# Attention and gated MLP on one core: how ScalarE and VectorE share the PSUM banks of the score blocks

## The chip, the cores and the metric

The kernel runs on one core of a Trainium2 chip. The metric is the device time of one execution in microseconds. Before the change the median of 14 runs is 795.35 us (791.35 to 800.95).

## The reference, cut to what matters

Two branches read the same `x` (2048 tokens of 512): an attention with 32 query heads of 16 that share one key and one value head, and a gated MLP with a 2048 x 2048 mixing matrix over the tokens. A sigmoid gate per token mixes them.

```python
q = (x @ wq) as 32 heads of 16;  k = x @ wk;  v = x @ wv        # one k and one v for all heads
scores = einsum('bhqd,bkd->bhqk', q, k) * 16 ** -0.5             # 32 x 2048 x 2048
a = softmax(scores) @ v  -> [2048, 512] @ wo
z = gelu(x @ w_in);  z1 = z[..., :688];  z2 = layernorm(z[..., 688:])
b = (z1 * (w_sp @ z2 + b_sp)) @ w_out
out = g * a + (1 - g) * b            # g = sigmoid((x * gate_w).sum(-1))
```

## The kernel before, in words

**Score blocks.** The attention is cut into 32 units of 64 score blocks, 2048 in all. A block is 128 keys x 512 columns, one PSUM bank of float32. Its matmul contracts over 32 rows only and uses one of the four row groups of the TensorE array (`s_mm`, recorded at L286); blocks of different row groups that stand next to each other run together. A *burst* is a group of such matmuls written for one exp.

**Two engines turn scores into weights.** ScalarE takes several banks at once and writes exp as bfloat16 to a slot of `P` (`exp_op`, L575; seven slots). VectorE takes one bank at a time: `d_A` (L599, "dA") evacuates it as an affine function in float16 to `X`, and for each batch of four blocks six polynomial steps on 1,024 columns follow (`d_poly`: square L607, add L609, square L611, each twice). VectorE's blocks thus get a polynomial in place of exp, and a small correction per unit (the `MC` and `CC` matmuls) adds what is missing. Which block goes to which engine is not fixed by hand.

**P times V.** TensorE multiplies the weights of either engine with `V` into bank 6 (`pv_mm`, L286, 128*32 tiles), four column groups beside each other. At the end of a unit VectorE transposes bank 6 (L623), and GpSimd divides by the sums (L629 to L635).

**The rest.** All projections, the mixing matmuls and the output go through bank 7 with an evacuation by VectorE (`Group` objects; L469, L476, L358, L523, L552 and others). ScalarE's gelus come in one piece near 272 us (L484, L508). To keep TensorE's clock up, matmuls on `ones` that nobody reads are put in where its load is low (`keep_pick`).

**PSUM.** Eight banks of 512 columns. Before the change, banks 0 to 2 and 3 to 4 are ScalarE's two slots, filled in turn with three and with two blocks; bank 5 (`BD`) is VectorE's; 6 (`BO`) is P times V and 7 (`BM`) everything else. Bank 5 also serves one of the last output tiles.

**Who sets the order.** A planner written in Python runs while the kernel is built. It follows TensorE, ScalarE and VectorE with a cost for each operation, asks `pe_pick`, `act_pick` and `dve_pick` for what could run next, and takes the ready candidate of the lowest priority number. The order that comes out is fixed for each engine; on the chip the engines wait for each other by semaphores, and every engine works strictly in that order. TensorE's candidates are: a ScalarE burst (priority 0, once the exp two bursts back is done), a lone VectorE block (1, unless a ScalarE burst is due within `SOON` = 300 ns), P times V (2, or 0.5 under pressure) and the groups (3). If bank 5 is free when a ScalarE burst is emitted, VectorE's block is put behind it. `dve_pick` takes evacuations first (0), then the unit ends (1) and small work (2), then dA (3), then the polynomial steps (4).

A batch for VectorE is taken from the upper end of a unit's key blocks, ScalarE takes them from the lower end, and at most 28 of the 64 blocks of a unit can go to VectorE (`NMAX`, `RMIN`).

Of the kernel before, what the change touches and what calls it, by code (L numbers as in the profile page):

```python
# [7 lines left out]
ACT = mybir.ActivationFunctionType  # L8
# [31 lines left out]
RLAST = 14  # L40
PVMIN = 8
PRESS = 1
SOON = 300
KEEP = 7.5
LOW = 6.0
MMARG = 250.0
# [106 lines left out]
def build_kernel(nc, x_d, wq_d, wk_d, wv_d, wo_d, win_d, wsp_d, bsp_d, wout_d, gw_d, out_d):  # L153
    es = ExitStack()
    with es:
# [7 lines left out]
        def bank(b, n=512, off=0):  # L163
            return ps[:, 512 * b + off:512 * b + off + n]

        BD = 5
        BO = 6
        BM = 7
        EB = ((0, 3), (3, 2))

        def bkey(b):
            return ("sc", 0) if b < 3 else ("sc", 1) if b < 5 else ("bk", b)

        xT = sb("xT", [128, 4, S], B16)
        wq = sb("wq", [128, 4, D], B16)
# [395 lines left out]
               rk + [("Q", (u // 2) % NQ)], [bkey(b)], tp=(32 * g, 0), tag="S")  # L571

        def exp_op(k, n):
            b0, _ = EB[k % 2]
            op("act", lambda a: a.activation(P[:, k % NP, 0:512 * n], ps[:, 512 * b0:512 * (b0 + n)], ACT.Exp),  # L575
               r=[("sc", k % 2)], w=[("P", k % NP)], tag="exp")

        pvn = {}

# [15 lines left out]

        pvt = {}

        def d_A(m, i):
            op("dve", lambda v: v.tensor_scalar(X[:, m % NX, 512 * i:512 * i + 512], bank(BD), PA, PB, ALU.mult, ALU.add),  # L599
               r=[("bk", BD)], w=[("X", m % NX, i * 2 // DB)], tag="dA")  # L600

        def d_poly(m):
            res = []
# [60 lines left out]


        for i in range(12):
            mm(bank(3 + i % 2), ones[:, 0:128], ones[:], True, True, ["ones"], [("sc", 1)], tag="warm")
        for dt in range(4):
            k_mm(0, dt, BM)
        k_ev(0, BM)  # L670
        for dt in range(4):
            q_mm(0, dt, BD)
        op("act", lambda a: a.activation(QA[:, 0, :], bank(BD), ACT.Copy), r=[("bk", BD)], w=[("Q", 0)], tag="Qev")
        op("dve", lambda v: v.tensor_scalar(wvg[:, :, 16:32], wk_sb[:], 0.25, None, ALU.mult), r=["wk"], w=["wvk"])
        op("dve", lambda v: v.tensor_copy(gw_rep[:], wvg[:, :, 32:33].broadcast_to([128, 4, 128])), r=["gw"], w=["gwr"])
        op("dve", lambda v: v.tensor_scalar(nmf[:], pidx[:], 0.0, None, ALU.is_ge), r=["pidx"], w=["nmf"])
# [36 lines left out]
        order = [(n // 4, n % 4) for n in range(64)]  # L713
        st_ = {"ua": 0, "kf": 0, "ke": 0, "pu": 0}
        stepb, sdone, edone, slot_left = {}, {}, {-1: 0.0, -2: 0.0}, {}
        dbank = {"free": 9500.0, "blk": None, "ready": None}
        batches = []
        cur = {"m": None, "gs": []}
        pd_left, bdone, xfree = {}, {}, {}
# [41 lines left out]
        def d_block(now, used):  # L761

            if not cur["gs"] and not new_batch(now):
                return None
            m = cur["m"]
            u, kt = batches[m]
            fr = [g for g in cur["gs"] if g not in used]
            if used and not fr:
                return None
            g = fr[0] if fr else cur["gs"][0]  # L770

            def take():
                cur["gs"].remove(g)
                i = cur["i"]
                cur["i"] += 1
                s_mm(BD, (u, kt, g))
                dbank["blk"] = (m, i, (u, kt, g))
            return take

        def sw(kind):  # L780
# [2 lines left out]
        def pe_pick(now):  # L783
            k = st_["kf"]
            ua = unit_for_act()
            cands = []
            dfree = dbank["blk"] is None and dbank["free"] + LAT <= now
            soon = False
            if ua < NU and edone.get(k - 2) is not None:
                nb = EB[k % 2][1]  # L790
                bl = []
                t = edone[k - 2] + (LAT if k >= 2 else 0)
                u = ua
                lo = units[u]["lo"]
                while len(bl) < nb and u < NU:
                    if lo >= units[u]["hi"]:
                        u += 1
                        if u < NU:
                            lo = units[u]["lo"]
                        continue  # L800
                    kt, g = order[lo]
                    r = when(("Q", u // 2), ("K", 0, kt // 4) if u % 2 == 0 else "K1")
                    if r is None:
                        break
                    if bl and r > max(t, now):
                        break
                    t = max(t, r)
                    bl.append((u, kt, g))
                    lo += 1
                if bl:  # L810
                    soon = t < now + SOON

                    def emit():
                        T["now"] = now
                        for i_, blk in enumerate(bl):
                            s_mm(EB[k % 2][0] + i_, blk)
                            units[blk[0]]["lo"] += 1
                        stepb[k] = bl
                        st_["kf"] += 1
                        unit_for_act()  # L820
                        if dfree:
                            tk = d_block(now, [b[2] for b in bl])
                            if tk:
                                tk()
                                dbank["new"] = True

                    def fin(t_end):
                        sdone[k] = t_end + LAT
                        if dbank.pop("new", None):
                            dbank["ready"] = t_end + LAT  # L830
                    cands.append((t, 0, sw("S") + 226, emit, fin, "S"))

            if dbank["blk"] is None and not soon:
                tk = d_block(now, ())
                if tk:
                    def fin2(t_end):
                        dbank["ready"] = t_end + LAT
                    cands.append((dbank["free"] + LAT, 1, sw("S") + 216, tk, fin2, "S"))

            pu = st_["pu"]  # L840
            if pu < NU:
# [105 lines left out]

        last_pe = {"kind": ""}
        tl_state = {12: 0, 13: 0}
        tl_bank = {12: BM, 13: BD}  # L950

        def keep_pick(now):

            while load and load[0][0] < now - 3400:
                load.popleft()
            have = sum(w_ for _, w_ in load)
            if have >= KEEP or st_["pu"] >= NU:
                return None
            if misc["cur"] is None and misc["free"] + LAT <= now and not tl_state[12]:
                b = BM  # L960
            elif dbank["blk"] is None and dbank["free"] + LAT <= now and not tl_state[13]:
                b = BD
            else:
                return None

            def emit():
                after = [pg.ops["dve"][-1]] if gel_on and gel else []
                mm(bank(b), ones[:, 0:128], ones[:], True, True, ["ones"], [("bk", b)], tag="keep", after=after)
            return (now, 1.5 if have < LOW else 9, C512 + sw("M"), emit, None, "M")

        def tail_pick(now):

            if st_["ua"] < NU - 2 or main or fins or ns or qs or misc["cur"] is not None or when(("OT", 3, 2), *[("u", ft, 3) for ft in range(6)]) is None:
                return None
            for t2 in (12, 13):
                if tl_state[t2] >= 9:
                    continue
                if t2 == 12:
                    ok = misc["free"] + LAT <= now
                else:  # L980
                    ok = st_["ua"] >= NU and not cur["gs"] and dbank["blk"] is None and dbank["free"] + LAT <= now
                if not ok:
                    continue

                def emit():
                    i = tl_state[t2]
                    if i < 6:
                        yb_mm(t2, i, tl_bank[t2])
                    else:
                        wo_mm(t2, i - 6, tl_bank[t2])  # L990
                    tl_state[t2] += 1
                return (now, 3, C512 + sw("M"), emit, None, "M")
            return None
# [67 lines left out]
        def dve_pick(now):  # L1061
            cands = []
            for q, pr in ((evac_q, 0), (norm_q, 1), (dve_q, 2)):
                if q:
# [11 lines left out]
                        if d_:  # L1076
                            d_(t_end + LAT)
                    cands.append((t, pr, c_, e, f))
            if dbank["blk"] is not None and dbank["ready"] is not None:
                m, i_, blk = dbank["blk"]  # L1080

                def e1():
                    d_A(m, i_)
                    bblk.setdefault(m, []).append(blk)

                def f1(t_end):
                    dbank["blk"] = None
                    dbank["ready"] = None
                    dbank["free"] = t_end
                    if i_ == DB - 1:  # L1090
                        ops_ = d_poly(m)
                        for z, (c_, f_) in enumerate(ops_):
                            polyq.append((c_, f_, m, z - 4 if z >= 4 else None))
                cands.append((dbank["ready"], 3, 601, e1, f1))
            if polyq:
                cp_, fp_, mp, last = polyq[0]

# [21 lines left out]
        while True:  # L1119
# [25 lines left out]
                if idle_rounds > 300:  # L1145
                    break
            free[eng] = min(nxt + [now + 200.0])
        assert st_["pu"] == NU and not (first or qs or ns or main or fins or gel or dve_q or evac_q or norm_q or polyq or act_q), \
            (st_, len(first), len(qs), len(ns), len(main), len(fins), len(gel), len(dve_q), len(evac_q), len(norm_q), len(polyq))
        if INFO is not None:  # L1150
            print({"est": tend, "busy": busy, "batches": len(batches), "n": [(64 - u["hi"]) // 4 for u in units], "tail": (tl_state, tl_bank)}, nc.sbuf_bytes_remaining)
# [5 lines left out]
                else:  # L1157
                    wo_mm(t2, i - 6, tl_bank[t2])
        for t2 in (14, 15):
            tl_bank[t2] = EB[st_["kf"] % 2][0] + (t2 - 14)  # L1160
        for t2 in (14, 12, 15, 13):
            wo_mm(t2, 3, tl_bank[t2], first=t2 >= 14)
        for t2 in (14, 12, 15, 13):
# [172 lines left out]
```

## Time and profile before

| what | value |
|---|---|
| median of 14 runs | 795.35 us |
| profiled execution | 792.48 us, span 790.7 us |
| granted TensorE clock | 0.993 |
| TensorE busy | 721.0 us (91%) |
| VectorE busy | 737.9 us (93%) |
| ScalarE busy | 765.6 us (97%) |
| first exp starts, last exp ends | 10.2 us, 781.0 us |

The span is from the first to the last instruction; the execution's own time is 1.8 us longer. PE is TensorE's matmul, PEld its weight load, DVE VectorE, ACT ScalarE, POOL GpSimd. A group's line gives line, engine, operation, output<-input, shapes and count; then busy time and mean duration of one; then the idle time of the engine just before them and what ended it. On ScalarE and VectorE an instruction's row overlaps the next one's by about 0.1 us, so sums of durations exceed busy times.

### The profile page before, as it was taken

To read this page: it belongs to the slowest core of one execution; us is meant where nothing else is said; L and a number is where in the kernel's file an instruction comes from. 1 tells how busy PE (TensorE), PEld (TensorE's weight loads), DVE (VectorE), ACT (ScalarE), POOL (GpSimd) and SP (SyncE) were. 2 spreads that over 40 slices of the span, in tenths; PEclk is the share of its full clock that TensorE was granted. 3 is DMA by queue.
4 is the path that set the end of the run, shared out by engine and by line. 5 is a ranking of instruction groups with operands and counts; after the bars stand their busy time and mean duration, and the time that the engine had idled before them with its cause. 6 is when DMAs were issued, how large, how long until landed. Compare 5 with 4: busy or idle time off the path is not lost.

```text
span 790.7 us, 13960 instructions
## 1 busy us (share of the span) xinstructions
PE 721.0 (91%) x5356; PEld 203.7 (26%) x5448; DVE 737.9 (93%) x1370; ACT 765.6 (97%) x669; POOL 135.7 (17%) x111
## 2 busy tenths in 40 slices
PE   7889999898999878999999999999999999999997
PEld 2222222222222222222222222222222222222221
DVE  3789999999999999999999899999999999899996
ACT  5999999999999999999999999999999999999995
POOL 3111101221120104211012111101112211111220
PEclk9899999999999999999999999999999999999999
DMA  9710000000000000000050000041000023000000
GB/s 192 171 28 1 1 1 1 1 1 2 1 1 1 2 0 1 1 1 1 1 121 15 1 1 1 1 81 47 7 2 1 1 54 68 14 1 2 2 1 30
DMA packets 49050, 16.99 MB, mean 21 GB/s; under 512 B 44130, under 2 KB 48914, under 8 KB 48979
## 3 DMA queue, kind: packets, MB, share of 16 engines
q1 hardware_dynamic: 46066, 15.10, 9.0%
q10 hardware_dynamic: 2784, 0.69, 0.5%
q8 instruction: 44, 0.72, 0.4%
q0 software_dynamic: 128, 0.26, 0.2%
q14 instruction: 28, 0.22, 0.1%
HBM read 3.20 MB, written 2.10 MB: 7 GB/s over the span
## 4 chain that ended last, share of the span: by engine, by line
PE 36%; DVE 28%; ACT 21%; issue 14%; DMA 1%; SPq 0%; ACTq 0%; DVEq 0%
PE ps L286 24%; ACT P L575 20%; PE ps L285 12%; DVE X L599 10%; DVE X L607 4%; DVE X L611 3%; DVE X L609 3%; DVE bst L490 2%; DMA xT<-in_A_x_dram 1%; DVE z L469 1%; DVE z L476 1%; DVE z L500 1%; DVE T L623 1%; DVE mv L492 0%; DVE OT L638 0%
## 5 line engine op out<-in xcount | busy, mean ns | idle before, releaser
L575 ACT ACTIVATE P<-ps 128x1536 bf16<-128x1536 f32 (+1 forms) x648 | 739.4, 1286 | 8.8 <-PE ps L286 7.1
L286 PE MATMUL ps<-QA,KA 32*128 32x512 bf16 x2048 | 335.7, 385 | 42.0 <-ACT P L575 23.3
L599 DVE TENSOR_SCALAR X<-ps 128x512 f16<-128x512 f32 x428 | 290.6, 679 | 25.4 <-PE ps L286 24.5
L629 POOL TENSOR_TENSOR rc<-T,mone 128x16 f32<-128x16 f32 x31 | 93.5, 3018 | 565.6 <-DVE T L623 565.6
L286 PE MATMUL ps<-P,V 128*32 128x512 bf16 x1620 | 160.8, 386 | 1.1 <-issue 0.8
L286 PEld LDWEIGHTS ps<-QA,KA 32*128 32x128 bf16 x2048 | 84.1, 91 | 300.1 <-ACT P L575 189.0
L611 DVE TENSOR_TENSOR X<-X 128x1024 bf16<-128x1024 f16 x214 | 144.4, 687 | 0.0
L607 DVE TENSOR_TENSOR X<-X 128x1024 f16<-128x1024 f16 x214 | 142.5, 685 | 0.0
L285 PE MATMUL ps<-wT,z 128*128 128x512 bf16 x348 | 108.5, 384 | 2.5 <-issue 2.1
L609 DVE TENSOR_SCALAR X<-X 128x1024 f16<-128x1024 f16 x214 | 85.4, 425 | 0.0
L286 PE MATMUL ps<-X,V 128*32 128x512 bf16 x428 | 69.9, 385 | 0.3 <-DVE T L623 0.2
L286 PEld LDWEIGHTS ps<-P,V 128*32 128x32 bf16 x1620 | 33.0, 94 | 60.0 <-issue 58.0
L285 PEld LDWEIGHTS ps<-wT,z 128*128 128x128 bf16 x384 | 29.4, 97 | 64.1 <-issue 55.5
L285 PE MATMUL ps<-ones 128*128 128x512 bf16 x101 | 34.9, 418 | 10.1 <-DVE bst L490 3.8
L285 PE MATMUL ps<-win,xT 128*128 128x344 bf16 x128 | 29.9, 314 | 1.0 <-DVE z L476 0.7
L285 PE MATMUL ps<-wout,z 128*128 128x512 bf16 x84 | 27.8, 385 | 1.1 <-issue 0.8
L285 PE MATMUL ps<-xT,win 128*128 128x512 bf16 x84 | 27.4, 385 | 0.7 <-issue 0.5
L623 DVE STREAM_TRANSPOSE T<-ps 128x512 f32<-128x512 f32 x32 | 22.6, 706 | 2.2 <-PE ps L286 2.2
L635 POOL TENSOR_TENSOR Tn<-T,rcg 128x256 bf16<-128x256 f32 x31 | 20.8, 670 | 2.4
L285 PE MATMUL ps<-xT,wq 128*128 128x512 bf16 x56 | 19.3, 397 | 0.8 <-issue 0.6
L285 PEld LDWEIGHTS ps<-ones 128*128 128x128 bf16 x113 | 10.3, 102 | 36.4 <-DVE bst L490 11.2
L286 PEld LDWEIGHTS ps<-X,V 128*32 128x32 bf16 x428 | 15.9, 94 | 14.3 <-issue 10.9
(102 smaller groups left out, 304.2 us busy)
## 6 DMA issues: line engine op xcount, KB each, us to landing
out_dram<-outsb SPq DMA_DIRECT2D x15, 128.0 KB, 2.2
win<-in_B_w_in_dram SPq DMA_DIRECT2D x2, 688.0 KB, 5.6
wout<-in_B_w_out_dram SPq DMA_DIRECT2D x1, 640.0 KB, 9.0
wo<-in_A_wo_dram SPq DMA_DIRECT2D x1, 512.0 KB, 6.7
wq<-in_A_wq_dram ACTq DMA_DIRECT2D x1, 384.0 KB, 9.3
wT<-in_B_w_sp_dram SPq DMA_TRANSPOSE x16, 4.6
KA<-KA POOLq DMA_DIRECT2D x4, 64.0 KB, 3.8
wq<-in_A_wq_dram ACTq DMA_DIRECT2D x1, 128.0 KB, 4.0
```

Source lines behind the costliest of these rows:

```text
L285: return t.matmul(dst, lhsT, rhs, start=start, stop=stop)
L286: return t.matmul(dst, lhsT, rhs, start=start, stop=stop, tile_position=tp)
L469: ev = lambda: op("dve", lambda v: v.tensor_copy(z1[:, ft, 512 * tc:512 * tc + 512], bank(BM)), r=[BMK], w=[("z1", ft)], tag="z1ev")
L490: dve_q.append((520, lambda st=st, h=h: op("dve", lambda v: v.bn_stats(bst[:, st, h, :], z2[:, FH * st + 344 * h:FH * st + 344 * h + 344]) ...
L575: op("act", lambda a: a.activation(P[:, k % NP, 0:512 * n], ps[:, 512 * b0:512 * (b0 + n)], ACT.Exp), r=[("sc", k % 2)], w=[("P", k % NP)] ...
L599: op("dve", lambda v: v.tensor_scalar(X[:, m % NX, 512 * i:512 * i + 512], bank(BD), PA, PB, ALU.mult, ALU.add), r=[("bk", BD)], w=[("X", ...
L607: res.append((C2, lambda x=x, k=k: op("dve", lambda v: v.tensor_tensor(x, x, x, ALU.mult), r=[k], w=[k], tag="dU")))
L609: res.append((C4, lambda x=x, k=k: op("dve", lambda v: v.tensor_scalar(x, x, PC, None, ALU.add), r=[k], w=[k], tag="dV")))
L611: res.append((C2, lambda x=x, k=k, p_=p_, kp=kp: op("dve", lambda v: v.tensor_tensor(p_, x, x, ALU.mult), r=[k], w=[kp], tag="dW")))
L623: o("dve", lambda v: v.transpose(T1[:], bank(BO)), r=[("bk", BO)], w=["T1"], tag="T1")
L629: o("pool", lambda g: g.tensor_tensor(rc[:].unsqueeze(2), lsum, mone[:].unsqueeze(2), ALU.pow), r=["T1", "mone"], w=["rc"], tag="rc")
L635: o(e, lambda v: v.tensor_tensor(tn, t1[:, :, 0:16], s_[:].unsqueeze(2).broadcast_to([128, 16, 16]), ALU.mult), r=["T1", k], w=[("Tn", pr, ...
```

## The change

Banks 0 to 2 and 3 to 5 become two slots of three banks, filled in turn. Each bank has its own key for the waits; before, the banks of a slot had one in common. A burst always has three blocks. When it is emitted and VectorE has at most `DAQ` = 1 evacuations and at most `DPQ` = 8 polynomial steps queued, the third bank of the slot is given to a VectorE block of another row group, and the exp has two banks; otherwise the exp has all three. A slot is filled again when both the exp and, where there was one, the dA of two bursts back are done. Lone VectorE bursts are gone, and `SOON` with them. dA gets priority -1, ahead of all other VectorE work. Keep-alive matmuls use bank 7 alone, and the late output tile takes the third bank of a free slot. Line numbers after L43 move by one at first (L599 becomes L600).

```diff
-SOON = 300
+DAQ = 1
+DPQ = 8
+APRI = -1.0
...
-        BD = 5
-        EB = ((0, 3), (3, 2))
+        EB = (0, 3)
         def bkey(b):
-            return ("sc", 0) if b < 3 else ("sc", 1) if b < 5 else ("bk", b)
+            return ("bk", b)
...
         def exp_op(k, n):
-            b0, _ = EB[k % 2]
+            b0 = EB[k % 2]
             op("act", lambda a: a.activation(P[:, k % NP, 0:512 * n], ps[:, 512 * b0:512 * (b0 + n)], ACT.Exp),
-               r=[("sc", k % 2)], w=[("P", k % NP)], tag="exp")
+               r=[bkey(b0 + i) for i in range(n)], w=[("P", k % NP)], tag="exp")
...
-        def d_A(m, i):
-            op("dve", lambda v: v.tensor_scalar(X[...], bank(BD), PA, PB, ALU.mult, ALU.add), r=[("bk", BD)], ...)
+        def d_A(m, i, b):
+            op("dve", lambda v: v.tensor_scalar(X[...], bank(b), PA, PB, ALU.mult, ALU.add), r=[bkey(b)], ...)
...  # pe_pick
-            if ua < NU and edone.get(k - 2) is not None:
-                nb = EB[k % 2][1]
+            if ua < NU and edone.get(k - 2) is not None and ddone.get(k - 2) is not None:
                 bl = []
-                t = edone[k - 2] + (LAT if k >= 2 else 0)
+                t = max(edone[k - 2], ddone[k - 2]) + (LAT if k >= 2 else 0)
-                while len(bl) < nb and u < NU:
+                while len(bl) < 3 and u < NU:
...
                     def emit():
+                        b0 = EB[k % 2]
+                        tk = None
+                        if len(da_q) <= DAQ and len(polyq) <= DPQ:
+                            tk = d_block(now, [b[2] for b in bl[:2]])
+                        if tk:
+                            del bl[2:]
                         for i_, blk in enumerate(bl):
-                            s_mm(EB[k % 2][0] + i_, blk)
+                            s_mm(b0 + i_, blk)
+                        if tk:
+                            new.append(tk(b0 + 2))
+                        else:
+                            ddone[k] = 0.0
-                        if dfree:
-                            tk = d_block(now, [b[2] for b in bl])
-                            if tk:
-                                tk()
...
-            if dbank["blk"] is None and not soon:
-                tk = d_block(now, ())
-                if tk:
-                    cands.append((dbank["free"] + LAT, 1, sw("S") + 216, tk, fin2, "S"))
...  # dve_pick
-                cands.append((dbank["ready"], 3, 601, e1, f1))
+                cands.append((t, APRI, 601, e1, f1))
```

## The prediction

> **What bounds the kernel now.** I read the page's engine shares first, then the groups kept apart by shape, the waits, one stretch of ScalarE's exps, and the timeline of VectorE beside TensorE. The page:
>
> ```profile
> span 790.7 us, 13960 instructions
> PE 721.0 (91%) x5356; PEld 203.7 (26%) x5448; DVE 737.9 (93%) x1370; ACT 765.6 (97%) x669; POOL 135.7 (17%) x111
> ```
>
> Three engines are nearly full, ScalarE most. The groups:
>
> ```profile
> L575 ACT ACTIVATE P<-ps 128x1536 bf16<-128x1536 f32 x324 | 484.8, 1496 | 8.1 <-PE ps L286 6.6
> L575 ACT ACTIVATE P<-ps 128x1024 bf16<-128x1024 f32 x324 | 348.4, 1075 | 0.7 <-PE ps L286 0.5
> L286 PE MATMUL ps<-QA,KA 32*128 32x512 bf16 x2048 | 335.7, 385 | 42.0 <-ACT P L575 23.3 <-DVE X L599 8.4 <-issue 4.6
> L599 DVE TENSOR_SCALAR X<-ps 128x512 f16<-128x512 f32 x428 | 290.6, 679 | 25.4 <-PE ps L286 24.5
> ```
>
> All 2048 score blocks are there: 324x3 + 324x2 = 1620 on ScalarE, 428 on VectorE. The two exp groups add up to 833 us, more than the span, since one exp's row overlaps the next, so the price of an exp is the distance of starts. In this stretch hardly anything waits:
>
> ```profile
> L575 ACT ACTIVATE P<-ps x20: 1018/1354/1672, 726.0 to 747.5; 128x1536 bf16<-128x1536 f32 x10, 128x1024 bf16<-128x1024 f32 x10
> ```
>
> 19 steps in 21.4 us; single starts in the trace lie 1,330 ns apart after a three-bank exp and 904 after a two-bank one (10x1.330 + 9x0.904 = 21.44). A bank is 426 ns, the fixed part 52. From the first exp (10.2 us) to the end of the last (781.0) ScalarE thus needs 324x2.234 = 723.8 us, plus 23.7 for gelus, table loads and small operations. The remaining 23 us are late starts, which the page mostly hides in the overlap (it shows 8.8 idle). By the starts, 20.0 us of them follow two-bank exps (62 ns on average) and 3.4 follow three-bank ones: after a two-bank exp TensorE has only 904 ns to refill the other slot. In 15.5 of the 20 TensorE reached that burst over 100 ns after the slot was free. ScalarE sets the end; TensorE's arrival sets its waits.
>
> The waits, and VectorE's single bank in the timeline:
>
> ```profile
> PEld ps L286 <- ACT P L575: 189.0, 469, 1.2
> PEld ps L286 <- DVE X L599: 51.8, 155, 1.5
> DVE X L599 <- PE ps L286: 24.5, 34, 2.0
> ```
> ```profile
> 404.69 0.67 DVE L599 TENSOR_SCALAR X<-ps 128x512 f16<-128x512 f32 x1
> 405.42 0.38 PE L286 MATMUL ps<-QA,KA 32*128 32x512 bf16 x1 [0.36 <-DVE X L599]
> 405.84 0.69 DVE L599 TENSOR_SCALAR X<-ps 128x512 f16<-128x512 f32 x1 [0.48 <-PE ps L286]
> 406.45 0.68 DVE L607 TENSOR_TENSOR X<-X 128x1024 f16<-128x1024 f16 x1
> 407.05 0.69 DVE L599 TENSOR_SCALAR X<-ps 128x512 f16<-128x512 f32 x1
> ```
>
> VectorE empties its bank, TensorE refills it with one lone matmul, and VectorE stands idle meanwhile. Its starts are 0.60 us apart (dA 601 ns, the two products 599 each, the sum 332), so a score block costs it 601 + (599+332+599)/2 = 1,366 ns. The least that all its work needs, by such distances, is 724.7 us; it ends at 787.1, so it waits about 61 us: 18 in the first 40 us (mostly for K), 3 in the tail, 41 between. By the starts, 32 of them are ahead of dA (the page shows 25.4).
>
> **ScalarE.** The built order of the changed kernel has 234 exps of three banks and 449 of two, 1600 blocks, with 448 on VectorE. 234x1.330 + 449x0.904 = 717.1 us, against 723.8: -6.7 (20 blocks fewer are -8.5, 35 more fixed parts +1.8). [...]
>
> The floor of the span by ScalarE is 10.2 + 717.1 + 23.7 + 9.7 (what follows the last exp) = 760.7 us, to which late starts come. Short windows grow from 324 to 449. No row shows the new burst, so I bound the loss per window by the nearest ones: 11 ns (that behind three-bank exps), and about 200 (the mean of the windows that were late at all, 94 of 321). I take 52, near the 62 of the same window length, less a sixth for TensorE's relief (next part): 449x0.052 + 2.5 for the long windows = 26, ScalarE's path 787. At 62 ns it is 791; break-even with 790.7 is 61 ns.
>
> **TensorE.** Before, bank 5 was often filled alone: the score matmuls form 852 waves (neighbours in different row groups, which run together), 197 of them a lone bank-5 matmul; after, 682, one such. A lone wave takes 0.31 us to the next kind of work in the timeline: 170x0.31 = -53 us. Keep-alive matmuls rise from 113 to 155, +42x0.31 = +13. Net -40 us, off the path: it buys earlier arrival at bursts, counted above with 10 of 62 ns; between 0 and 48 (62 less the 15.5 of 20.0 us in which TensorE was late) it could be anything, and 10 is nearer to nothing because 40 us are 6% of TensorE's 721. P-V waves stay (599 to 595), as do projections, DMAs, GpSimd and the SP queue. The granted clock is 0.993 and TensorE stays as dense, so nothing is taken for it.
>
> **VectorE.** 20 more blocks: 20x1.366 = +27.3 us, making 752.0 us of work. That must be paid from its 61 us of waits. In the built order the queue of polynomial steps was empty ahead of 113 of 428 dA before, and is empty ahead of 7 of 448 after: with two banks and that backlog it hardly starves. Bounds on what goes: nothing, or all 32 ahead of dA and the some 7 ahead of evacuations (L623, L454, L358, L523, L492). I take 28 of the 32 and 3 of the 7, since where it has a backlog it is full already today, as in this stretch (third pair of columns: DVE busy, operations); that removes 31. The span by VectorE is 790.7 + 27.3 - 31 = 787.
>
> ```profile
> core 0: us, PE busy (x) PEld busy (x) DVE busy (x) ACT busy (x) POOL busy (x), PEclk, DMA share, GB/s
> 60.00:100.00 40.00, 37.12 (x294) 11.25 (x296) 40.00 (x77) 39.35 (x35) 7.68 (x6) 1.00 0.00 1
> ```
>
> The order also moves the tail: two batches of polynomial steps, and not one, follow the last dA, so VectorE and not the last exp leads to the end; this is inside its sum.
>
> **The added wait.** A slot is refilled when both engines have left it. dA runs first of all VectorE work, but not in the middle of an operation: up to 0.60 us late, then 0.68 long, at most 1.28 us after its matmul, beside 0.904 for the exp. The third matmul waits on TensorE, and P-V waves, projections and the next burst stand behind it. ScalarE's own two matmuls go first, so its next exp is covered; if that cover fails the price is the first rival's.
>
> **Sum.** The span ends with the longer path; both give 787 us, -3.7 (-0.5%). The profiled run took 792.48, 1.8 over its span; the median of the runs is 795.35, 2.9 more. 787 + 1.8 + 2.9 = 791.7.
>
> **Rivals.** *A slot tied to two engines (slower).* VectorE at 98% runs behind, TensorE stands in front of a third bank, and the next exp comes late. Place: L287 score matmuls waiting for L600. Price: 449 windows at 80 instead of 52 ns, 760.7 + 35.9 + 2.5 = 799, median 804. It decides from 67 ns on (793.1 us). For it: 51.8 us of weight loads already wait on L599. Against: there are now two banks to wait for. Chance 0.33.
>
> *The waits only move (no change).* VectorE sheds 25 to 29 us of waits instead of 31 and pays 27 for its 20 blocks: 789 to 793, median 794 to 798. For it: VectorE's row cannot shrink, and a block costs it 1,366 ns to save ScalarE 426. Chance 0.12.
>
> *TensorE's relief pays in full (faster still).* Late starts fall to 40 ns per window (ScalarE's path 781) and VectorE sheds 39: 779 to 781, median 784 to 786. Against: both must happen at once. Chance 0.07.
>
> *It doesn't do what it says.* Every burst may be shared, but 234 of 683 are not: 683 blocks would need 683x1.366 = 933 us of VectorE. That is already in the counts.
>
> **Numbers.** The forecast has 0.48. Faster by over 0.3% (about what a measurement of this kernel can tell from no change) needs a span under 788.3: that is the fast rival, 0.07, and 0.38 of the forecast's 0.48, together 0.45. Within 0.3% are the forecast's other 0.10 and 0.10 of the second rival, 0.20. Slower are the first rival and the second's last 0.02, 0.35. The range 784 to 804 runs from the fast rival's time to the slow one's; the forecast's own is 788 (ScalarE's windows at 45 ns and VectorE shedding 35: span 783) to 797 (either path at 792).
>
> **What would show it.** Right: VectorE 96 to 98% of the span, idle ahead of dA under 10 us (25.4 now), exp groups x234 and x449, ScalarE's share lower than 97%, no lone score matmul. Wrong: idle ahead of dA still over 20 us; more TensorE time waiting for L600 than 51.8 + 8.4 us together with ScalarE idle ahead of L576 over 20 us (the slow rival); a span under 780 would mean that VectorE's work was mis-summed.

## The result, and the profile after

The changed kernel takes 809.52 us (median of 10 runs, 802.38 to 813.28) against 795.57 (47 runs) of the kernel before. The ratio on record is 1.0159, 95% interval 1.0134 to 1.0183 (it is not the quotient of the two medians). It is slower by 14 us; 791.7 had been forecast, and 809.52 lies above the range. The profiled execution took 806.69 us with a span of 804.9, 14.2 more than before.

The page's head, with the engine shares, the granted clock in 40 slices and the shares of the chain that ended last:

```profile
span 804.9 us, 14176 instructions
...
PE 702.4 (87%) x5402; PEld 198.3 (25%) x5490; DVE 764.4 (95%) x1420; ACT 764.6 (95%) x704; POOL 139.6 (17%) x111
...
PEclk9799999999999999999999999999998999999986
...
DVE 53%; PE 21%; issue 11%; ACT 10%; DMA 2%; POOL 2%; ACTq 0%; DVEq 0%
```

Before, the chain's line read as follows:

```profile
PE 36%; DVE 28%; ACT 21%; issue 14%; DMA 1%; SPq 0%; ACTq 0%; DVEq 0%
```

The reader should see VectorE's share of the chain go from 28% to 53%, while its busy share rose only from 93 to 95%. The groups, kept apart by shape:

```profile
L576 ACT ACTIVATE P<-ps 128x1024 bf16<-128x1024 f32 x449 | 434.0, 1054 | 11.4 <-PE ps L287 9.1
L576 ACT ACTIVATE P<-ps 128x1536 bf16<-128x1536 f32 x234 | 329.4, 1474 | 10.5 <-PE ps L287 8.7
L600 DVE TENSOR_SCALAR X<-ps 128x512 f16<-128x512 f32 x448 | 299.5, 679 | 10.1 <-PE ps L287 4.4
```

The counts are those of the prediction (234, 449, 448). The idle time ahead of dA fell from 25.4 us to 10.1, and yet ScalarE now idles 21.9 us ahead of its exps instead of 8.8. TensorE's waits, after the change (what waits, for what; us in total, times, the longest):

```profile
PEld ps L287 <- DVE X L600: 15.2, 51, 0.9
...
PEld ps L286 <- DVE bst L491: 14.7, 25, 1.5
PEld ps L286 <- DVE z L477: 13.6, 27, 1.2
PEld ps L286 <- DVE z L470: 12.9, 22, 1.5
PEld ps L286 <- DVE z L524: 9.1, 16, 1.3
```

Before, the last four read:

```profile
PEld ps L285 <- DVE bst L490: 11.2, 21, 1.6
...
PEld ps L285 <- DVE z L476: 5.2, 15, 0.7
PEld ps L285 <- DVE z L469: 5.0, 11, 0.9
...
PEld ps L285 <- DVE z L523: 3.5, 9, 0.5
```

TensorE's wait for VectorE has changed its place. All its waits (weight loads and matmuls, lines added up) for dA went from 66.2 to 19.3 us; those for the evacuations of bank 7 and the other small work of VectorE (all that isn't `X` or `T`) went from 51.0 to 104.9. TensorE works in its order, so a burst that comes later in it stands behind such a wait: at 117.71 us a keep-alive's weight load starts after 1.27 us of waiting for L359, and the burst behind it, for which the profile shows no other wait, starts at 118.03.

By the starts of its instructions ScalarE's run can be added up: 10.2 us to the first exp + 717.1 of exps + 23.7 other work + 41.1 late starts + 12.5 after the last exp = 804.6. The late starts were 20.0 + 3.4 us before, and 9.7 us followed the last exp. VectorE's run: 751.0 us of work (724.7 before) + 49.2 of waits (62.3 before) + 4.5 after its last instruction = 804.7 (3.6 of such time before). Both sums describe the same run; which of the two engines makes the other late is not in them, and that is what the experiments had to tell.

A third suspect was the clock: stretches at half TensorE clock lasted 50.6 us in all, against 13.4 before (counted in the windows of 3.4 us).

### The profile page after: what moved, and what is told of

Same layout as the page of the kernel before. It is cut to its first block, busy times and chain, and to the rows that moved or that the text cites. A ratio compares the mean times of both kernels' runs of the same rounds, so it can differ in the third digit from the quotient of the medians.

```text
span 804.9 us, 14176 instructions
## 1 busy us (share of the span) xinstructions
PE 702.4 (87%) x5402; PEld 198.3 (25%) x5490; DVE 764.4 (95%) x1420; ACT 764.6 (95%) x704; POOL 139.6 (17%) x111
## 4 chain that ended last, share of the span: by engine, by line
DVE 53%; PE 21%; issue 11%; ACT 10%; DMA 2%; POOL 2%; ACTq 0%; DVEq 0%
DVE X L600 20%; PE ps L287 14%; ACT P L576 10%; DVE X L612 8%; DVE X L608 8%; PE ps L286 7%; DVE X L610 5%; DVE bst L491 2%; DMA KA<-KA 2%; POOL rc L630 2%; DVE T L624 1%; DVE z L470 1%; DVE z L477 1%; DMA wvg<-in_gate_w_dram 1%; DVE z L524 1%
## 5 line engine op out<-in xcount | busy, mean ns | idle before, releaser
L576 ACT ACTIVATE P<-ps 128x1024 bf16<-128x1024 f32 (+1 forms) x683 | 738.3, 1198 | 21.9 <-PE ps L287 17.9
L287 PE MATMUL ps<-QA,KA 32*128 32x512 bf16 x2048 | 295.8, 392 | 50.7 <-ACT P L576 40.1
L600 DVE TENSOR_SCALAR X<-ps 128x512 f16<-128x512 f32 x448 | 299.5, 679 | 10.1 <-PE ps L287 4.4
L287 PEld LDWEIGHTS ps<-QA,KA 32*128 32x128 bf16 x2048 | 76.2, 91 | 303.9 <-ACT P L576 224.9
L608 DVE TENSOR_TENSOR X<-X 128x1024 f16<-128x1024 f16 x224 | 150.2, 685 | 0.0
L612 DVE TENSOR_TENSOR X<-X 128x1024 bf16<-128x1024 f16 x224 | 148.5, 683 | 0.0
L287 PE MATMUL ps<-X,V 128*32 128x512 bf16 x448 | 80.0, 391 | 0.9 <-DVE T L624 0.4
L286 PE MATMUL ps<-ones 128*128 128x512 bf16 x140 | 46.5, 406 | 22.6 <-DVE bst L491 6.1
L287 PEld LDWEIGHTS ps<-X,V 128*32 128x32 bf16 x448 | 19.1, 95 | 21.1 <-issue 13.2
L286 PE MATMUL ps<-wo,OT 128*128 128x512 bf16 x61 | 19.6, 384 | 2.5 <-DVE OT L639 2.2
```

Of the source, the lines that this page charges most:

```text
L286: return t.matmul(dst, lhsT, rhs, start=start, stop=stop)
L287: return t.matmul(dst, lhsT, rhs, start=start, stop=stop, tile_position=tp)
L608: res.append((C2, lambda x=x, k=k: op("dve", lambda v: v.tensor_tensor(x, x, x, ALU.mult), r=[k], w=[k], tag="dU")))
L612: res.append((C2, lambda x=x, k=k, p_=p_, kp=kp: op("dve", lambda v: v.tensor_tensor(p_, x, x, ALU.mult), r=[k], w=[kp], tag="dW")))
```

## The experiments

In each, "exps" counts those of three and of two banks; late starts are ScalarE's after a two-bank exp at full clock; work and waits are VectorE's by the distances of starts. All ratios are to the kernel before on the same chip. A span is that of one profiled execution, a median or ratio that of all executions of a kernel; executions of one kernel differ by some us, so a difference of a few us counts only where the ratios show it too.

**1. The clock: keep-alives inside bursts, none at all, and dA after the evacuations.** The first suspicion was that TensorE, less dense without its lone score matmuls, loses its clock, and that this delays the bursts. The first kernel puts a keep-alive matmul into the still unwritten third bank of a shared slot where TensorE's recent load is low:

```diff
+KB = 9.0
...
                         if tk:
+                            while load and load[0][0] < now - 3400:
+                                load.popleft()
+                            if sum(w_ for _, w_ in load) < KB:
+                                mm(bank(b0 + 2), ones[:, 0:128], ones[:], True, True, ["ones"], [bkey(b0 + 2)], tag="keep")
                             new.append(tk(b0 + 2))
```

> The changed kernel with keep-alive matmuls on ones written into the third bank of a shared burst, between ScalarE's two blocks and VectorE's block, where TensorE's load is low: 126 of them, 262 keep-alives in all instead of 155; exps x234 and x449 as before. Theory 1 (the clock): 9.6 us of the added late exps and about 3 us of the longer end lie in the 50.6 us at half clock, 13.4 us before the change. Half clock falls below 25 us, the granted clock rises to 0.985 or more, the span falls from 804.9 by 8 to 13 us, to 792 to 797. Theory 2 (a slot tied to two engines): the clock is a companion; the new matmuls stand ahead of VectorE's block, so the span stays at 805 or grows to 810, even where the clock is higher.

Measured: 852.43 us, 1.0758 (1.0704 to 1.0811), span 847.9. Half clock 62.7 us, not fewer. Late starts 145 ns per short window instead of 62. The groups:

```profile
L577 ACT ACTIVATE P<-ps 128x1024 bf16<-128x1024 f32 x449 | 440.1, 1041 | 44.1 <-PE ps L288 41.9
L577 ACT ACTIVATE P<-ps 128x1536 bf16<-128x1536 f32 x234 | 328.8, 1461 | 15.3 <-PE ps L288 14.2
...
L601 DVE TENSOR_SCALAR X<-ps 128x512 f16<-128x512 f32 x448 | 304.3, 687 | 47.7 <-PE ps L288 41.4
```

Both engines now idle for TensorE. There are 262 keep-alives instead of 155, and 155 times, not 17, keep-alives stand between two score matmuls. The planner doesn't count those inside bursts when it sets the order, each takes some 0.3 us (an estimate, the prediction's 0.31 us for a lone wave) in front of a burst's end, and both consumers wait. Neither theory had allowed for this: the forecasts were 792 to 797 and 805 to 810. The experiment shows that late matmuls in a burst cost dearly in this order; of the clock it says nothing.

```diff
-KEEP = 7.5
-LOW = 6.0
+KEEP = 0.0
+LOW = 0.0
```

> The changed kernel without any keep-alive matmul in the steady part (12 at the start remain, 143 taken out); exps x234 and x449. Theory 1 (clock): half clock grows from 50.6 us to over 150 us, every further 40 us of it cost about 10 us, span over 825. Theory 2: TensorE has less to do and arrives sooner at the bursts, span 800 to 805.

Measured: 811.45 us, 1.0202 (1.0154 to 1.025), span 810.7, half clock 117.5 us. With 67 us more at half clock the span is 5.8 us longer, 0.09 us for each; by the medians it is 1.9 us, and the intervals of the two ratios overlap. At 0.09 the change's own 37 us more are some 3 of its 14.2 us, an estimate. It isn't a clean price: 143 matmuls are gone as well, and the order differs in places.

```diff
-APRI = -1.0
+APRI = 1.5
```

> The changed kernel with dA behind evacuations and unit ends (priority 1.5 and not -1) but ahead of the polynomial steps. Theory 1 (clock): the half-clock stretches come where bank 7 waits for its evacuation, so that neither projections nor keep-alives can run; evacuations come sooner, half clock falls to 20 to 35 us, span 794 to 801. Theory 2 (tied slot): dA ends later by up to 0.6 us, more of TensorE's time goes to waiting for L600 (15.2 us of weight loads now), span 808 to 815.

Measured: 808.12 us, 1.019 (1.0146 to 1.0233), the same span of 804.9. The planner now gave VectorE 452 blocks (756.3 us of work; exps 230/453). Half clock fell by 21 us; no time came of it. TensorE's waits for bank 7's evacuations and small work fell from 104.9 to 91.6 us, those for dA rose from 19.3 to 24.3, and the two-bank exps started 88 ns late. So the clock is out as the main cause. Two more numbers on record agree: one execution of the changed kernel had a granted clock of 0.834, where the others had 0.964 to 0.974, and took 809.71 us, where the median is 809.52; and the new layout with 84 additions left out (part 4) has 40.0 us at half clock and a span of 786.9. Letting other results of VectorE go first didn't help either, though its 5 us more work blur that second reading.

**2. Truer costs for the planner, with the keep-alives in bursts.** The planner counts an exp of one, two or three banks at 510, 940 or 1,346 ns; by the trace it is 904 for two and 1,330 for three. No run has an exp of one bank; its 480 is an estimate, 904 less the 426 of a bank.

```diff
-cands.append((t, 1, (0, 510, 940, 1346)[len(bl)], e2, f2))
+cands.append((t, 1, (0, 480, 904, 1330)[len(bl)], e2, f2))
...  # and the edit of the first kernel
```

> The kernel of the first run with the planner's exp costs set to what the trace shows (0.904 us for two banks, 1.330 for three, instead of 0.940 and 1.346): exps x246 and x437, 436 blocks on VectorE. Theory 1: VectorE's work is 12 blocks smaller (16.4 us), ScalarE's floor 3.8 us larger than in the changed kernel; the plan releases the slots when the chip does, fewer late arrivals: span 783 to 790, below both kernels. Theory 2 (tied slot): 437 short windows stay, the span is 795 to 803.

Measured: 824.34 us, 1.0361 (1.0313 to 1.0409), span 823.3: far over both forecasts and over the change, but 28 us under the first kernel. The costs changed the division of the blocks (exps 246/437, 436 blocks on VectorE, 735.7 us of work), so two things moved at once, and it doesn't tell them apart.

**3. VectorE's load alone.** The new theory: VectorE is over-full, and through TensorE's waits for it everything else is late. The rival: the slot that two engines must leave is what costs, and VectorE's load is beside the point. The same order was built with one of VectorE's steps left out, in both layouts: the "add" of each polynomial half batch (224 and 214 instructions; this part of the weights is then not computed).

```diff
-res.append((C4, lambda x=x, k=k: op("dve", lambda v: v.tensor_scalar(x, x, PC, None, ALU.add), ...)))
+res.append((C4, lambda: None))
```

> The changed kernel without VectorE's sum step (L610, 224 operations of 0.33 us, 74 us of VectorE's 751): that part of the polynomial is left out, the planner still counts it, so the order of all that remains is the same. Theory A (VectorE sets the end): VectorE needs 677 us and is no longer late; the span falls from 804.9 by 10 to 20 us, to 785 to 795, where ScalarE's path lies (760.7 plus about 27 us of late exps), and late exps after two-bank exps fall from 36 to 28 us. Theory B (TensorE's late arrivals and the clock set the end, VectorE only waits with them): 801 to 805.

> The kernel before with the same step left out (214 operations of L609, 71 us), same order. Theory A: VectorE isn't the bound there, but some lone refills of its bank come sooner: 787 to 791 us of span (790.7 now). Theory B: the same, 788 to 791. The two theories differ in the changed kernel; this run says what the step is worth where VectorE has room.

Measured: the new layout 782.73 us, 0.9859 (0.9815 to 0.9904), span 779.7; the old layout 789.71, 0.9934 (0.9909 to 0.9959), span 790.2. In the new layout TensorE's, ScalarE's and GpSimd's orders are those of the change, and 25 us are gone. The chain and then the groups of ScalarE, new layout without the step:

```profile
ACT 49%; issue 23%; PE 20%; DVE 4%; DMA 3%; POOL 1%; ACTq 0%; DVEq 0%
```
```profile
L576 ACT ACTIVATE P<-ps 128x1024 bf16<-128x1024 f32 x449 | 436.5, 1105 | 2.3 <-PE ps L287 1.5
L576 ACT ACTIVATE P<-ps 128x1536 bf16<-128x1536 f32 x234 | 335.2, 1525 | 5.1 <-PE ps L287 5.0
```

The same 683 exps now idle 7.4 us instead of 21.9, start 27 ns late instead of 62 after two banks, and lead the chain with 49%; VectorE has 4% of it. The gain is larger than theory A had it (785 to 795). With VectorE out of the way the new layout's span is 10.5 us shorter than the old's (7.0 by the medians).

**4. The reverse, and a smaller dose.** VectorE got extra work in the old layout (an addition on a scratch tile of 768 columns per batch, which nobody reads, 28.3 us in all); and in the new layout 84 of the 224 additions were left out (that part of the weights is not computed), so that VectorE's work is that of the kernel before. The planner knows of neither, so the order stays.

```diff
+            def f1():      # the kernel before: ahead of a batch's first step
+                op("dve", lambda v: v.tensor_scalar(scr[:], scr[:], 1.0, None, ALU.add), r=["scr"], w=["scr"])
+                f0()
...
+                if k[2] and m % 4 != 3:      # the changed kernel: an addition left out
+                    res.append((C4, lambda: None))
+                    continue
```

> The kernel before with one extra VectorE operation per batch on a scratch tile (107 of about 0.27 us, some 28 us in all, as much as the change adds), order otherwise the same. Theory A (VectorE's load is what the change pays for): the old layout pays for it too; of 39 us of VectorE's waits in the middle of the run some 13 go, as in the changed kernel, and the span grows by 8 to 15 us to 799 to 806. Theory B' (only a slot tied to two engines turns VectorE's load into time): the old layout takes it up in its waits, 790 to 794.

> The changed kernel with 84 of the 224 sum steps left out (28 us of VectorE's work, which brings it to the 724 us of the kernel before), order otherwise the same. Theory A: the span falls by 15 to 20 us, to 785 to 790, late exps after two-bank exps to about 35 ns; the layout itself is then worth 0 to 5 us against the kernel before. Theory B': the tied slot still costs, 796 to 802.

Measured: the old layout with more work 818.56 us, 1.0318 (1.0278 to 1.0358), span 816.0, 10 us above theory A's range; the new layout with less 788.79, 0.9937 (0.9912 to 0.9962), span 786.9. The chains, first of the old layout with more work, then of the new with less:

```profile
DVE 56%; PE 31%; issue 7%; ACT 4%; DMA 1%; SPq 0%; ACTq 0%; DVEq 0%
```
```profile
DVE 37%; PE 23%; ACT 21%; issue 15%; DMA 2%; POOL 2%; ACTq 0%; DVEq 0%
```

All six spans by VectorE's work, with the ratio of all executions behind each:

| VectorE's work, old / new | old layout | new layout |
|---|---|---|
| 654 / 678 us | 790.2 (0.9934) | 779.7 (0.9859) |
| 725 / 724 us | 790.7 (1) | 786.9 (0.9937) |
| 753 / 751 us | 816.0 (1.0318) | 804.9 (1.0159) |

This settles that VectorE's load is what the change pays for. The last 27.4 us of VectorE's work cost the new layout 18.0 us of span, and the last 28.3 cost the old one 25.3; the ratios give the same. Below some 725 us it costs little: by the spans 0.5 us for 71 in the old layout and 7.2 for 46 in the new one, by the ratios some 5 and 6 us. The rival is out: with the shared slots and the order unchanged the loss is gone, and the old layout, which has no shared slot, pays for the same load. The waits show the path with the order unchanged: at 678, 724 and 751 us of VectorE's work TensorE's waits for bank 7's evacuations and small work are 58.0, 79.1 and 104.9 us in the new layout, those for dA 7.7, 9.9 and 19.3. In the old layout the overload shows most at dA's own bank (all waits of TensorE for dA 109.7 us, from 66.2). Which of these waits makes an exp late was not isolated; part 1 took 13 us off those at bank 7, with 5 us more work, and gained nothing. The old layout's extra work stands in no plan, and part of its 25.3 us may be due to that; in part 5 the planner counts all of the work.

At equal work of VectorE the new layout's spans are 4 to 11 us shorter. That isn't what the layout is worth: ScalarE has 20 blocks fewer there, 6.7 us of exps, and VectorE can take them along at equal work only because additions are left out. Beyond this, at 724 us of work, 449 short windows lose about as much in all as 324 did (some 21 and 20 us).

**5. Fewer blocks for VectorE, by the costs or by the queue.** If this is so, the new layout should gain where the planner gives VectorE less. Two ways: truer costs (those of part 2, and a slot's release 75 ns later, tried in the old layout too), and a lower limit `DPQ` on the queued steps at which a burst is shared.

```diff
-DPQ = 8
+DPQ = 4        # alone and with the true costs; 6 with the costs; 3 alone
...
-                        edone[k] = t_end
+                        edone[k] = t_end + 75        # wherever the costs are changed
```

> The changed kernel with the planner's exp costs set to the distances of starts in the trace (0.904 and 1.330 us) and its release of a slot set 0.075 us after that (an exp's row is 0.14 us longer than the distance); exps x242 and x441, 440 blocks on VectorE. Theory A: VectorE's work is 8 blocks or 11 us smaller, ScalarE's floor 2.5 us larger: 790 to 797. Theory B: as many short windows (441) with the same late arrivals, 802 to 808.

> The changed kernel that shares a burst only while at most 4 polynomial steps are queued, not 8: 440 blocks on VectorE, exps x242 and x441. Theory A: VectorE needs 740 us; with the same waits of 49 the span falls by 11 us to 794, less what its shorter queue adds in waits: 794 to 800. Theory B: TensorE's arrivals are unchanged, 802 to 808.

> The kernel with the planner's true exp costs and later release, sharing only while at most 4 polynomial steps are queued: 428 blocks on VectorE as in the kernel before, exps x254 and x429 (ScalarE's floor 725.6 us, 1.8 more than before). Theory A: VectorE at 724 us has room; ScalarE's path is 10 + 725.6 + 23.7 + 10.5 + late starts of 17 to 22, so 787 to 792: equal to the kernel before or up to 0.5% faster. Theory B': 796 to 802.

> The same with at most 6 queued: 436 blocks on VectorE, exps x246 and x437. Theory A: VectorE 735 us plus waits of 48 and its 0.9 and 3.6 at the ends, 787; ScalarE's path 10 + 722.2 + 23.7 + 10.5 + 22 = 788: span 786 to 791. Theory B': 798 to 803.

> The changed kernel, planner costs as they were, sharing only while at most 3 polynomial steps are queued: 420 blocks on VectorE, exps x262 and x421. If VectorE's load alone made the change slower, VectorE at 713 us has room, late exps after two-bank exps are about 30 ns, and the span is ScalarE's path: 10 + 729.0 + 23.7 + 10.5 + 18 = 791, 788 to 794, equal to the kernel before. If the wrong costs matter by themselves, 796 to 800, where the 440-block version lay.

> The kernel before with the same two changes to the planner as the 428-block version of the changed kernel (exp costs 0.904 and 1.330 us, slots released 0.075 us later): 420 blocks on VectorE, exps x326 and x325. If the gain of that version over the kernel before is the layout's, this run shows none: ScalarE's floor rises to 727.4 us, VectorE's work falls to 714, span 789 to 795. If the gain is the costs', it is 784 to 788 here too.

| kernel | blocks on VectorE | its work, us | exps' least, us | late start after two banks, ns | span, us | median, us | ratio |
|---|---|---|---|---|---|---|---|
| the change | 448 | 751.0 | 717.1 | 62 | 804.9 | 809.52 | 1.0159 (1.0134 to 1.0183) |
| true costs | 440 | 739.9 | 720.5 | 40 | 792.5 | 797.65 | 1.0044 (1.0019 to 1.0069) |
| limit 4 | 440 | 740.7 | 720.5 | 55 | 796.7 | 801.02 | 1.0083 (1.0058 to 1.0108) |
| true costs, limit 6 | 436 | 734.1 | 722.2 | 31 | 787.8 | 791.93 | 0.9964 (0.9942 to 0.9986) |
| true costs, limit 4 | 428 | 723.3 | 725.6 | 29 | 788.7 | 789.22 | 0.9938 (0.9913 to 0.9962) |
| limit 3 | 420 | 714.5 | 729.0 | 39 | 799.1 | 801.28 | 1.0077 (1.0049 to 1.0105) |
| old layout, true costs | 420 | 714.1 | 727.4 | 32 | 799.8 | 802.54 | 1.0100 (1.0072 to 1.0128) |

At 440 blocks the truer costs are worth 4.2 us beyond the load: 792.5 against 796.7, with the same exps' least and the same work to 0.8 us. The lower limit alone doesn't reach the kernel before at all; limits 4 and 3 are both 0.8% slower. With truer costs and the limit at 4 the new layout beats both kernels: 789.22 us, 6.3 us under the kernel before on its chip. Its chain, and the page's group of dA:

```profile
ACT 48%; issue 22%; PE 15%; DVE 13%; DMA 1%; ACTq 0%; DVEq 0%
...
L600 DVE TENSOR_SCALAR X<-ps 128x512 f16<-128x512 f32 x428 | 288.1, 685 | 19.3 <-PE ps L287 15.2
```

VectorE idles twice as long ahead of dA as in the change (19.3 against 10.1 us), has 13% of the chain instead of 53%, and the kernel is faster. At the other end, with 420 blocks at limit 3, ScalarE binds: its exps alone need 729.0 us, 11.9 more than in the change, and VectorE waits 51 us in the middle. Its chain:

```profile
ACT 40%; issue 20%; PE 20%; DVE 16%; DMA 2%; POOL 0%; ACTq 0%; DVEq 0%
```

For this kernel the account by VectorE's load alone had forecast 788 to 794, and it missed: the span is 799.1, in the range that had been written down for the case that the wrong costs matter by themselves. The late starts are the difference, 25.2 us where 18 were forecast. So VectorE's load explains why the change is slower, and not every time in this table; the order that the planner's costs make has a price of its own.

What stays open is how much of 789.22 is the layout's and how much the costs'. The old layout with the same costs took 802.54, but its exps end at 780.6 us as before, and its loss is in the end of its order: 19.2 us follow the last exp instead of 9.7. It had been forecast at 789 to 795 or 784 to 788 and missed both, and it doesn't price the costs in the old layout.

## Why the prediction was wrong, point by point

- **VectorE's waits: the step that failed.** The work was right: 26.3 us more by the trace, 27.3 forecast. "That removes 31" was not. (The 61 us of waits were also 62.4 by the prediction's own 787.1 - 724.7.) VectorE's waits fell from 62.3 to 49.2 us, by 13: in the first 60 us from 20.4 to 19.3, between from 39.1 to 26.0, in the last part they rose from 2.8 to 3.9. Ahead of dA some 16 of the 32 us went, not 28, and elsewhere some 3 us were added, where 3 were to go. The forecast had left it 31.3 us of waits; the 17.9 more that it had are all that the path of 787 lacks to 804.9 (1.0 less work and 0.9 more behind its last instruction cancel). The evidence for "31" was the count of dA with an empty queue in the built order (7 of 448). The count was no measure of waits on the chip; why the waits stay although the plan has a backlog is open. In no run of the new layout did VectorE wait under 20.7 us in the middle, and in the overloaded old layout it waited 34.3.
- **ScalarE's late starts.** 52 ns per short window had been put down to the length of the window and TensorE's relief. Measured were 62 at full clock and 81 with the stretches at half clock, 36.2 us in all, and 4.9 after three banks: 41.1 where 26 were forecast. With the 2.8 more behind the last exp that, too, is the whole of the 17.9. But it is a consequence: the same exps in the same order start 35 ns late with 28 us less on VectorE, and 27 with 74 less. Without VectorE's overload the term would have been too dear, not too cheap.
- **ScalarE's floor and the exps** were as forecast, 717.1 us by the counts. **TensorE's relief** went the forecast way: no lone score matmul, and TensorE busy 18.6 us less, where the sum had 40; 39.3 us of its busy time, not 9.5, lay at half clock. A short window followed by another short one loses 47 ns, one in front of a three-bank burst 112.
- **The added wait** was covered, as said: exps held up by a dA that had not left the third bank lost 3.4 us in all.
- **The clock.** Nothing was taken for it; half clock rose by 37 us, worth some 3 us at most by the run without keep-alives, an estimate.
- **The rivals.** The first had the nearest time (a median of 804) and, with 80 ns per short window, nearly the price that came (81), but the wrong place, so this is luck: weight loads and matmuls waiting for L600 were to exceed 51.8 + 8.4 us and are 15.2 + 3.0. It was right that VectorE runs behind. The second, that VectorE sheds less of its waits than it takes on in work, has the mechanism that happened; it allowed for 25 to 29 us shed, not 13, and so ended at no change.
- **The marks** that were to show the forecast right were there or nearly so: the groups x234 and x449, ScalarE at 95%, no lone score matmul; VectorE at 95% where 96 to 98 had been said, idle ahead of dA 10.1 us where under 10. They can't tell the two cases apart, because rows overlap (dA's is 679 ns long, its starts 601 apart) and an engine with a backlog hardly idles by the page (VectorE's 10.1 us ahead of dA, beside 49.2 of waits in all by the starts). The sign of the slower case was ScalarE idle ahead of L576 over 20 us together with more waiting for L600; the first half came (21.9), the second did not.

## What to carry to other kernels

An engine whose results TensorE waits for in its order needs a reserve: here VectorE's work cost little up to some 725 of 790 us (at most some 7 us for 46 to 71 us of work), and beyond it about two thirds to nine tenths of every added microsecond came out in the time, before its waits had gone. So when a change moves work to such an engine, don't pay for it from its waits; ask who stands in a strict order behind its later results (here TensorE, whose waits grew most at bank 7), and vary that engine's load alone, in both layouts, before blaming the layout. And when a layout changes, set the division of work anew: here 428 to 436 blocks instead of 448 turned 1.6% slower into 0.4 to 0.6% faster, along with truer costs in the planner; fewer blocks alone left it 0.8% slower.

## What the runs showed of the hardware that was not expected

**TensorE's clock halved while TensorE worked.** Two windows after the change, near the end (us, TensorE busy and its instructions, granted clock, DMA share, GB/s):

```profile
776.80:780.20 3.40, 2.01 (x19) 1.00 0.00 0
780.20:783.60 3.40, 2.60 (x17) 0.51 0.00 0
```

TensorE was busy 2.01 of 3.40 us in the first, its longest idle stretch was 0.95 us, and the second ran at 0.51 of the clock. So in this case a window that was 59% busy by the profile, at full clock, preceded the half clock.

**The half clock was cheap here.** With 117.5 instead of 50.6 us of it the span was 5.8 us longer (the median 1.9), although TensorE is busy for 87% of the span in the change; 143 keep-alive matmuls were gone in that run as well. An execution of the change at a granted clock of 0.834 took 809.71 us, where the median is 809.52.

**VectorE did not fill up.** VectorE never had less than 44 us of waits in all in any of these kernels, with up to 756 us of work in a span of 805. Why at least 20 us of them stay between the start and the end of the run was not tried and is open.
